# Which queue carries which half of wk: a change to the first three transfers of a gated attention and SwiGLU kernel

## The chip, the cores and the metric

The kernel runs on one core of one Trainium2 chip. The metric is the device time of one execution in microseconds; "the median" is that over several executions without a profile. The profile is of one further execution, and times in it are counted from the start of its span. The engines are called PE (TensorE; PEld is its weight load), ACT (ScalarE), DVE (VectorE), POOL (GpSimd) and SP (SyncE, which issues transfers here and computes nothing).

## The reference

The inputs are bf16. With x of 2048 rows (tokens) and 512 columns the kernel computes

```python
qkv = x @ wqkv                     # 512 x 1536, split in q, k, v; 32 heads of 16
phi = lambda t: where(t > 0, t + 1, exp(t)) + 1e-6
kv  = einsum("bhsd,bhse->bhde", phi(k), v);  z = phi(k).sum over tokens
o   = (phi(q) @ kv) / (phi(q) . z + 1e-6)
a   = o @ wo                       # linear attention
b   = (silu(x @ w1) * (x @ w3)) @ w2     # 512 -> 1376 -> 512
g   = sigmoid((x * gate_w).sum(-1))
out = g * a + (1 - g) * b
```

## The kernel before

Tokens are worked in 16 tiles of 128 (index t), four tiles to a block of 512 (index tb). Everything stays in SBUF: x in its own layout (`x_sb`), x transposed (`xT`), and all weights. The order of PE's instructions is written out by hand (`manual_schedule` for PE, line 152); on the other engines a scheduler keeps the order in which the instructions are written where nothing forces another.

**Loads.** All loads but one are issued on SP's queue (`dq = nc.sync`), in this order: the first two token tiles of x (256 KB, line 84), the second half of wk (`wk_sb[:, 2:4, :]`, 256 KB, line 86), then transposing loads of x into `xT` (lines 89 and 93) in turn with the remaining tiles of `x_sb` (line 98), then wq, the small weights, wv, w1, w3, wo and w2 (lines 99 to 114). The exception is the first half of wk (`wk_sb[:, 0:2, :]`, 256 KB, line 85), which is issued on ACT's queue. "Half" counts the four chunks of 128 input columns over which a matmul of k accumulates: the first half holds chunks 0 and 1, the second chunks 2 and 3. Behind that transfer ACT runs a one-element exp into a tile `pre` (line 88) that nothing reads: it makes ACT load its table of functions early (ACT_TABLE_LOAD).

A transfer raises a completion counter; eight counters are used in turn by all transfers, so that a later transfer on the same counter waits for the earlier one to have landed.

**The start on PE.** Nine matmuls on constants (`emit_warm`, line 163) run first; they need no transfer. Then the first two token tiles are transposed on PE itself (`emit_xT`, line 176; eight transposes, from `x_sb`), and copied to `xT` by DVE (chunks 0 and 1 of each tile, line 181) and by ACT (chunks 2 and 3, line 183). The matmuls of k for these tiles follow in this order (line 379; kc is the chunk, t the tile):

```python
for kc, t in ((0, 0), (1, 0), (0, 1), (1, 1), (2, 0), (3, 0)):
    emit_k_mm(k0[t], t, kc)
```

The first four need the first half of wk alone, the fifth is the first to need the second half. The remaining two chunks of tile 1 and the tiles 2 and 3 follow, whose `xT` comes by the transposing load of line 89.

**The rest.** phi (line 140) is an exp on ACT and two operations on DVE. For the later tiles PE takes x^T phi(k) (`emit_xp`) and the next k in turn, then q, the remainder columns, the feed-forward matmuls (`emit_ffn`) and the outputs (`emit_out`), whose results SP stores.

Of the kernel before, what the change touches and what calls it, by code (L numbers as in the profile page):

```python
# [8 lines left out]
ACT = mybir.ActivationFunctionType  # L9
ALU = mybir.AluOpType  # L10
AX = mybir.AxisListType
ENG = mybir.EngineType
FP32 = mybir.dt.float32
# [4 lines left out]
def kernel(  # L18
# [12 lines left out]
    nc = tc.nc  # L31
    P = nc.NUM_PARTITIONS

    Bb, S, D = A_x.shape
# [29 lines left out]
    x_sb = consts.tile([P, NT, D], BF16, name="x_sb")  # L64
    xT = consts.tile([P, KC, S], BF16, name="xT")
    wk_sb = consts.tile([P, KC, D], BF16, name="wk_sb")
# [9 lines left out]
    wqkv_r = A_wqkv.rearrange("(kc d) n -> d kc n", d=P)  # L76
# [3 lines left out]
    dq = nc.sync  # L80
    TF = 2
    x_first = x2d[0 : TF * P, :].rearrange("(p j) d -> p j d", j=TF)
    out_first = out2d[0 : TF * P, :].rearrange("(p j) d -> j p d", j=TF)
    dq.dma_start(out=x_sb[:, 0:TF, :], in_=x_first)
    nc.scalar.dma_start(out=wk_sb[:, 0:2, :], in_=wqkv_r[:, 0:2, D : 2 * D])
    dq.dma_start(out=wk_sb[:, 2:4, :], in_=wqkv_r[:, 2:4, D : 2 * D])
    pre = consts.tile([1, 1], FP32, name="pre")
    nc.scalar.activation(out=pre[:], in_=nc.const_aps.tensor(0.0, [1, 1], FP32), func=ACT.Exp)
    dq.dma_start(
        out=xT[:, :, TF * P : TB], in_=x2d[TF * P : TB, :], transpose=True  # L90
    )
    for tb in range(1, NTB):
        dq.dma_start(
            out=xT[:, :, tb * TB : (tb + 1) * TB], in_=x2d[tb * TB : (tb + 1) * TB, :],
# [7 lines left out]
    with nc.allow_non_contiguous_dma(reason="one gate weight per partition and chunk"):  # L102
        dq.dma_start(
            out=wr_sb[:, :, 2 * FR : NR], in_=gate_w.rearrange("(kc d o) -> d kc o", d=P, o=1)
# [7 lines left out]
    for fcs in (slice(0, FC // 2), slice(FC // 2, FC)):  # L112
# [9 lines left out]
        out=bm, in_=bm, pattern=[[-Dh, HPC], [0, Dh]], compare_op=ALU.is_ge, fill=0.0,  # L122
# [3 lines left out]
        out=bm, in_=bm, pattern=[[Dh, HPC], [0, Dh]], compare_op=ALU.is_ge, fill=0.0,  # L126
# [288 lines left out]
    for c in range(KC):  # L415
# [7 lines left out]
        out=kvT_sb[:], in0=kvT_ps[:],  # L423
# [65 lines left out]
```

## Time and profile before

| What | Value |
|---|---|
| Median of 4 executions without a profile | 179.43 us (179.22 to 179.96) |
| The profiled execution's own time | 180.21 us |
| Its span, first to last instruction | 178.4 us |
| PE busy | 173.8 us |
| ACT busy / DVE busy / POOL busy | 66.0 / 117.8 / 63.2 us |
| SP's queue: share of the 16 transfer engines' time | 30.4%, 14.72 MB |
| ACT's queue: share of the same | 0.4%, 0.26 MB |
| First x pair, issue to landing | 3.1 us |
| wk's first half, on ACT | 3.6 us |
| wk's second half, on SP | 4.0 us |

"Busy" counts the time in which an engine has an instruction in work; PE's matmuls overlap one another, so a busy PE is not PE at its peak. The profiled execution took 1.8 us more than its span, which lie around the first and last instruction. It was 0.8 us longer than the median, so differences are taken against its own time and then put on the median.

### The profile page before, as it was taken

The page shows a single profiled execution, that of the slowest core. Times are in us where ns is not written, and L with a number is a line of the kernel's source. Part 1 is how long each engine was busy: PE and PEld are TensorE (multiplying, and loading weights), DVE is VectorE, ACT ScalarE, POOL GpSimd, SP SyncE. Part 2 cuts the span into 40 slices and gives each one's busy share as a digit, 9 for nine tenths or more (in the row PEclk, how much of TensorE's full clock was granted, in tenths as well). Part 3 has the DMA queues.
Part 4 walks back from the last instruction along what each step waited for, and adds up shares of the span by engine and source line. Part 5 has one row for each costly group of instructions (what it writes and reads, how often), then busy time and mean ns, then how long its engine had stood idle before and what let it go on. Part 6 is the DMA issues. An engine that isn't in the chain of part 4 may idle for free.

```text
span 178.4 us, 2453 instructions
## 1 busy us (share of the span) xinstructions
PE 173.8 (97%) x868; PEld 84.1 (47%) x884; DVE 117.8 (66%) x203; ACT 66.0 (37%) x124; POOL 63.2 (35%) x71
## 2 busy tenths in 40 slices
PE   8999999999999999999999999999999999999993
PEld 3444444474444545444454544444545444444463
DVE  0397667898998837498786375978754669776000
ACT  3542323467532333342333333342433323341221
POOL 5087765867363323262003232620032328100000
PEclk9999999999999999999999999999999999999999
DMA  4999999921014011124000111240001022300011
GB/s 167 242 276 231 296 288 362 351 91 28 9 21 99 0 44 33 44 59 88 0 0 11 37 37 37 59 90 6 0 7 63 11 66 62 60 0 0 29 40 52
DMA packets 30252, 15.14 MB, mean 85 GB/s; under 512 B 20672, under 2 KB 30112, under 8 KB 30240
## 3 DMA queue, kind: packets, MB, share of 16 engines
q1 hardware_dynamic: 29968, 14.72, 30.4%
q10 hardware_dynamic: 272, 0.26, 0.4%
q8 instruction: 7, 0.11, 0.3%
q14 instruction: 5, 0.04, 0.1%
HBM read 8.42 MB, written 2.10 MB: 59 GB/s over the span
## 4 chain that ended last, share of the span: by engine, by line
PE 97%; issue 1%; DVE 0%; DVEq 0%
PE o_ps L357 19%; PE up_ps L320 19%; PE gate_ps L312 19%; PE o_ps L348 8%; PE XP L206 8%; PE q_ps L219 8%; PE k_ps L186 6%; PE r_ps L243 3%; PE k L186 2%; PE o_ps L352 2%; PE warm L163 2%; PE xTp L176 1%; PE kvT_ps L418 1%; PE W_ps L440 0%; PE z_ps L431 0%
## 5 line engine op out<-in xcount | busy, mean ns | idle before, releaser
L312 PE MATMUL gate_ps<-xT,w_sb 128*128 128x512 bf16 x157 | 40.8, 379 | 0.1
L320 PE MATMUL up_ps<-xT,w_sb 128*128 128x512 bf16 x157 | 40.6, 379 | 0.2
L227 POOL TENSOR_TENSOR qz<-pq,z_sb 128x512 f32<-128x512 bf16 x16 | 18.5, 1163 | 59.7 <-DVE pq L147 58.4
L325 ACT ACTIVATE th<-gate_ps 128x512 bf16<-128x512 f32 x40 | 23.9, 597 | 37.9 <-PE gate_ps L312 36.4
L357 PE MATMUL o_ps<-w_sb,hT 128*128 128x512 bf16 (+2 forms) x177 | 37.4, 355 | 0.2
L327 DVE SCALAR_TENSOR_TENSOR gs<-th,gate_ps 128x512 bf16<-128x512 bf16 x40 | 27.3, 682 | 5.6 <-ACT th L325 5.4
L330 DVE TENSOR_TENSOR hT<-up_ps,gs 128x512 bf16<-128x512 f32 x40 | 27.6, 691 | 3.8
L144 DVE TENSOR_SCALAR phi_m<-phi_e 128x512 bf16<-128x512 bf16 x32 | 14.1, 440 | 22.0 <-ACT phi_e L142 22.0
L357 PEld LDWEIGHTS <-hT 128*128 128x128 bf16 x180 | 16.8, 97 | 18.0
L320 PEld LDWEIGHTS <-w_sb 128*128 128x128 bf16 x160 | 15.6, 98 | 18.9
L312 PEld LDWEIGHTS <-w_sb 128*128 128x128 bf16 x160 | 15.6, 98 | 18.7
L362 ACT ACTIVATE o_out<-o_ps,omg 128x512 bf16<-128x512 f32 (+2 forms) x17 | 11.1, 656 | 30.4 <-PE o_ps L357 30.4
L292 POOL TENSOR_TENSOR pqn<-pq,rden 128x512 bf16<-128x512 bf16 x16 | 16.5, 1055 | 14.0 <-DVE rden L285 11.7
L196 POOL TENSOR_TENSOR pks<-pks,pk_sb 128x512 f32<-128x512 f32 x15 | 17.4, 1161 | 7.3 <-DVE pk_sb L147 6.7
L348 PE MATMUL o_ps<-W_sb,pqT 128*128 128x512 bf16 (+2 forms) x70 | 16.7, 355 | 0.1
L230 DVE TENSOR_REDUCE den<-qz 128x32 f32<-128x512 f32 x16 | 10.9, 684 | 8.6 <-POOL qz L227 8.5
L206 PE MATMUL XP<-pk_sb,x_sb 128*128 128x512 bf16 x62 | 16.2, 379 | 0.1
L219 PE MATMUL q_ps<-wq_sb,xT 128*128 128x512 bf16 x61 | 16.1, 379 | 0.1
L142 ACT ACTIVATE phi_e<-k_ps 128x512 bf16<-128x512 f32 x12 | 7.2, 597 | 14.4 <-PE k_ps L186 14.4
L142 ACT ACTIVATE phi_e<-q_ps 128x512 bf16<-128x512 f32 x16 | 9.6, 597 | 7.8 <-PE q_ps L219 6.7
L186 PE MATMUL k_ps<-wk_sb,xT 128*128 128x512 bf16 x48 | 12.3, 379 | 0.0
L147 DVE SCALAR_TENSOR_TENSOR pq<-q_ps,phi_m 128x512 bf16<-128x512 f32 x16 | 11.1, 691 | 0.5
(59 smaller groups left out, 118.5 us busy)
## 6 DMA issues: line engine op xcount, KB each, us to landing
w_sb<-in_B_w_dram SPq DMA_DIRECT2D x6, 640.0 KB, 9.7
out_dram<-o_out SPq DMA_DIRECT2D x15, 128.0 KB, 1.9
x_sb<-in_A_x_dram SPq DMA_DIRECT2D x2, 512.0 KB, 4.4
x_sb<-in_A_x_dram SPq DMA_DIRECT2D x1, 768.0 KB, 5.2
wq_sb<-in_A_wqkv_dram SPq DMA_DIRECT2D x1, 512.0 KB, 5.2
wv_sb<-in_A_wqkv_dram SPq DMA_DIRECT2D x1, 512.0 KB, 6.6
wo_sb<-in_A_wo_dram SPq DMA_DIRECT2D x1, 512.0 KB, 11.3
wk_sb<-in_A_wqkv_dram ACTq DMA_DIRECT2D x1, 256.0 KB, 3.6
```

What stands on the lines that cost most here:

```text
L186: nc.tensor.matmul(k_ps[:], lhsT=xT[:, kc, t * P : (t + 1) * P], rhs=wk_sb[:, kc, :], start=(kc == 0), stop=(kc == KC - 1),)
L196: nc.gpsimd.tensor_add(pks[:], pks[:], pk_sb[:, t, :])
L206: nc.tensor.matmul(XP_ps[dc][:], lhsT=x_sb[:, t, dc * P : (dc + 1) * P], rhs=pk_sb[:, t, :], start=(t == 0), stop=(t == NT - 1),)
L219: nc.tensor.matmul(q_ps[:], lhsT=xT[:, kc, ts_tok], rhs=wq_sb[:, kc, :], start=(kc == 0), stop=(kc == KC - 1),)
L227: nc.gpsimd.tensor_tensor(out=qz[:], in0=st[tb, "pq"][:, tt, :], in1=z_sb[:], op=ALU.mult)
L312: nc.tensor.matmul(gate_ps[:], lhsT=w1_sb[:, kc, fsl], rhs=xT[:, kc, tok_sl], start=(kc == 0), stop=(kc == KC - 1),)
L320: nc.tensor.matmul(up_ps[:], lhsT=w3_sb[:, kc, fsl], rhs=xT[:, kc, tok_sl], start=(kc == 0), stop=(kc == KC - 1),)
L325: nc.scalar.activation(out=th[:], in_=gate_ps[:], func=ACT.Tanh, scale=0.5)
L327: nc.vector.scalar_tensor_tensor(out=gs[:], in0=th[:], scalar=1.0, in1=gate_ps[:], op0=ALU.add, op1=ALU.mult)
L330: nc.vector.tensor_tensor(out=st[tb, "hT"][:, fc, :], in0=up_ps[:], in1=gs[:], op=ALU.mult)
L348: nc.tensor.matmul(o_ps[:], lhsT=st[tb, "pqT"][:, c, tsl], rhs=W_sb[:, c, a:b], start=(c == 0), stop=False,)
L357: nc.tensor.matmul(o_ps[:], lhsT=st[tb, "hT"][:, fc, tsl], rhs=w2_sb[:, fc, a:b], start=False, stop=(fc == FC - 1),)
```

## The change

The two halves of wk change queues. SP issues the first pair of x tiles and then wk's first half; ACT runs the one-element exp, with the table load ahead of it, and then issues wk's second half. A `manual_schedule` for ACT holds these in the written order. Sizes, destinations and all later transfers are the same, and no wait is added on ACT. The order of instructions of PE, DVE and POOL is the same; PE's first k matmul now waits for SP's second transfer, its fifth for ACT's.

```diff
-    dq.dma_start(out=x_sb[:, 0:TF, :], in_=x_first)
-    nc.scalar.dma_start(out=wk_sb[:, 0:2, :], in_=wqkv_r[:, 0:2, D : 2 * D])
-    dq.dma_start(out=wk_sb[:, 2:4, :], in_=wqkv_r[:, 2:4, D : 2 * D])
     pre = consts.tile([1, 1], FP32, name="pre")
-    nc.scalar.activation(out=pre[:], in_=nc.const_aps.tensor(0.0, [1, 1], FP32), func=ACT.Exp)
+    with tc.manual_schedule(engines={ENG.Activation}):
+        dq.dma_start(out=x_sb[:, 0:TF, :], in_=x_first)
+        dq.dma_start(out=wk_sb[:, 0:2, :], in_=wqkv_r[:, 0:2, D : 2 * D])
+        nc.scalar.activation(
+            out=pre[:], in_=nc.const_aps.tensor(0.0, [1, 1], FP32), func=ACT.Exp
+        )
+        nc.scalar.dma_start(out=wk_sb[:, 2:4, :], in_=wqkv_r[:, 2:4, D : 2 * D])
     dq.dma_start(
         out=xT[:, :, TF * P : TB], in_=x2d[TF * P : TB, :], transpose=True
     )
```

The lines behind the change move down by three: line 89 of the kernel before is line 92 after, line 176 is 179, line 186 is 189.

## The prediction

> **What bounds the kernel now.** I read the page first, for the engine that sets the end, and then the first microseconds of the timeline, because the change touches only the first three transfers and the table load.
>
> ```profile
> span 178.4 us, 2453 instructions
> PE 173.8 (97%) x868; PEld 84.1 (47%) x884; DVE 117.8 (66%) x203; ACT 66.0 (37%) x124; POOL 63.2 (35%) x71
> PEclk9999999999999999999999999999999999999999
> PE 97%; issue 1%; DVE 0%; DVEq 0%
> ```
>
> TensorE is busy 173.8 of 178.4 us and carries 97% of the chain that ended last. The 4.6 us that are left are 0.84 us before its first matmul, 2.9 us after its last one (the last output) and under a microsecond in between. So a delay of TensorE at the start is handed on whole to the end, and only what TensorE waits for is worth anything. The next view is the timeline from 0 (start us, duration, engine, line, operation, [idle before <- releaser]).
>
> ```profile
> 0.80 0.45 ACTq L85 DMA_DIRECT2D wk_sb<-in_A_wqkv_dram  x1
> 0.81 0.40 SPq L84 DMA_DIRECT2D x_sb<-in_A_x_dram  x1
> 0.84 3.04 PE L163 MATMUL warm<-const-bfloat16-1.0 128*128 128x512 bf16 x9 [0.84 <-PEq L473]
> ...
> 1.27 0.41 SPq L86 DMA_DIRECT2D wk_sb<-in_A_wqkv_dram  x1
> 1.28 1.28 ACT L88 ACT_TABLE_LOAD   x1 [1.28 <-PEq L473]
> ...
> 1.73 1.32 SPq L89 DMA_TRANSPOSE xT<-in_A_x_dram  x1
> ...
> 2.57 0.20 ACT L88 ACTIVATE pre<-const-float32-0.0 1x1 f32<-1x1 f32 x1
> ...
> 3.91 0.77 PEld L176 LDWEIGHTS <-x_sb 128*128 128x128 bf16 x8 [0.29 <-DMA x_sb<-in_A_x_dram]
> ...
> 4.55 0.81 ACT L183 ACTIVATE xT<-xTp 128x256 bf16<-128x256 bf16 x2 [1.78 <-PE xTp L176]
> 4.69 0.20 PEld L186 LDWEIGHTS <-xT 128*128 128x128 bf16 x2
> 4.74 4.35 PE L186 MATMUL k<-wk_sb,xT 128*128 128x512 bf16 x16
> ```
>
> Today the first half of wk leaves from ACT at 0.80 beside x on SP at 0.81, and the second half follows on SP at 1.27. The DMA view gives issue to landing (KB each, median us):
>
> ```profile
> wk_sb<-in_A_wqkv_dram ACTq DMA_DIRECT2D x1, 256.0 KB, 3.6
> x_sb<-in_A_x_dram SPq DMA_DIRECT2D x1, 256.0 KB, 3.1
> wk_sb<-in_A_wqkv_dram SPq DMA_DIRECT2D x1, 256.0 KB, 4.0
> ```
>
> So x lands at 0.81+3.1 = 3.91, wk's first half at 0.80+3.6 = 4.40, its second half at 1.27+4.0 = 5.27. TensorE takes x at 3.91, the moment it lands (the 0.29 us wait). It takes wk's first half at 4.74, 0.34 us after that landed, and wk's second half with the fifth k matmul. That one starts at 6.34, 1.07 us after the landing, as TensorE's weight loads show:
>
> ```profile
> 5.17 0.15 PEld L186 LDWEIGHTS <-xT 128*128 128x128 bf16 x1 [0.28 <-DVE xT L181]
> 5.60 0.15 PEld L186 LDWEIGHTS <-xT 128*128 128x128 bf16 x1 [0.28 <-issue]
> 6.02 0.15 PEld L186 LDWEIGHTS <-xT 128*128 128x128 bf16 x1 [0.28 <-issue]
> 6.34 1.18 PEld L186 LDWEIGHTS <-xT 128*128 128x128 bf16 x6 [0.17 <-issue]
> ```
>
> Two matmuls stand 0.43 us apart up to 6.02, and from 6.34 on six loads take 1.18 us, which is 0.22 us apart. TensorE runs its first matmuls at half rate and goes to full rate at about 6.2 in this execution, although the PEclk row reads 9 from the first slice.
>
> **The change part by part.**
> *ACT's queue.* The table load goes to the head and starts where the first ACT instruction starts now, 0.80 instead of 1.28; 1.28 us of load and 0.20 of pre then end at 2.29 instead of 2.77. ACT's next work is the xT copy at 4.55, so that costs and brings nothing; if the cover went, it would be at most the load's 1.28 us. The moved DMA issue (0.45 us) has the same cover. Neither it nor the activation before it waits for a semaphore.
>
> *When ACT's copy really leaves* is the question. No row of before has a DMA issue behind work of ACT's engine. From one side it leaves after pre ends, at 2.30. From the other, ACT's sequencer hands load and pre to the engine and goes on: a DMA issue is the sequencer's own work. Its pace is 0.03 us (issue ended at 1.25, load began at 1.28), so the issue would start at about 0.9. Two rows lie nearer to this end: pre starts 0.01 us after the load ends, so it already stood ready, and the trace's semaphore instructions of ACT, which the views leave out, stand while its engine works (one at 8.274, inside an ACTIVATE from 8.27 to 8.87). I take 0.9: "behind the table load" then holds in the program's order but not in time.
>
> *SP's queue.* x at 0.81 as now; then wk's first half in the place, size and time (1.27) of the second half now; the transposes at 1.73 and everything after keep their places. The later SP transfers that reuse these completion counters start at 11.67, long after all three have landed. POOL, DVE and TensorE keep their order; TensorE's first k matmul now waits for SP's second transfer and its fifth for ACT's.
>
> *The cost at 0.9.* The two halves of wk have changed places. ACT's copy leaves 0.1 us later than now, still 0.37 ahead of SP's second one, so it is served second again and lands about 4.5, where nobody needs it before 6.34. SP's second transfer is now the half that TensorE needs at 4.74, and by its row it lands at 5.27; 5.29 with the 0.02 of an issue. Behind the waiting matmul stand all later TensorE work and ACT's first exp; the stall is 5.29−4.74 = 0.55 us. x gains nothing, since ACT's copy runs beside it as now. Bounds of the landing: 1.27+3.6 = 4.87 (stall 0.13) and 1.27+4.0+0.1 = 5.37 (0.63). I take the row of the same queue and place.
>
> *What 0.55 us is worth.* If the rate rises at 6.2 anyway, the 0.55 us displace half-rate work: 6.2−4.74 = 1.46 us at half rate did 0.73 of full-rate work, 6.2−5.29 = 0.91 do 0.46, a loss of 0.28. If the rate is already up by 4.74, or rises later by the stall, the loss is 0.55. The profiled execution took 180.21 us, 0.78 above the median; if that is its slow start, half a microsecond per microsecond, the median one rose about 1.6 us earlier, near 4.7. Both ends are near, so I take 0.4.
>
> *The sum.* 0 (ACT) + 0 (x) + 0.4 (stall) = +0.4 on the profiled 180.21, that is 180.6; on the median, 179.43+0.4 = 179.83. Nothing later takes it back: TensorE has no wait of that size left.
>
> *A rule against the change.* The rows of ACT's and SP's first issues overlap (0.80 to 1.25 and 0.81 to 1.21), and neither is longer than SP's lone one (0.41) by more than 0.04, so no long exclusion is seen between plain copies. The Trainium skill, Perfetto Trace Analysis, section Per-instruction lifecycle, says that descriptor generation is one block that an issuing queue locks for itself until all its descriptors are made. By that, a late ACT issue falls into SP's transposes and waits them out; by the row it does not. By the rule the sum would be that of the third rival.
>
> **The rivals.**
> *1. The copy does wait for pre.* Then ACT's DMA leaves at 2.30 and wk's first half follows x at once on SP, without ACT's copy beside them. It would land as ACT's first copy does now, 4.40, bounds 4.37 (1.27+3.1) and 5.27; x could land up to 0.2 earlier of the 0.29 waited. The second half lands at 2.30+3.1 = 5.4 to 2.30+4.0 = 6.3, needed at 6.34, or at 4.74+4×0.22 = 5.6 where the rate is up early. So −0.2 to +0.3, about 179.4: not slower. For it speaks the change's wording and that ACT's work is in program order; against it the two rows above.
>
> *2. The stall keeps the clock down.* In this trace the full rate came 5.4 us after the first matmul (0.84), through one gap of 0.29 us ending at 3.91. If a gap of 0.55 begins the count anew, where 0.29 did not, the rise comes between 5.29+(6.2−3.91) = 7.6 and 5.29+5.4 = 10.7; at half rate that is (7.6−6.2)/2 = 0.7 to 2.25 us on top of 0.28: 180.4 to 181.9. Against it: TensorE would still be busy for most of that stretch. It decides from the gap length at which a stretch stops counting as busy, and no row shows that length. The skill's TensorE: Matmul & The Clock Gate, Part 1, has a free-running window of about 3.4 us that must be busy; a lost window would cost half of it, 1.7, for an estimated 181.4.
>
> *3. ACT's issue at 2.30 is held by SP's transposes.* They are issued from 1.73 to 3.05 and from 3.10 to 5.91. ACT's copy would leave at 3.05 or at 5.91, land between 6.15 and 9.9, and stall the fifth matmul by 0 to 3.6 us: 179.4 to 183.0. Against it the overlapping issues.
>
> **How the numbers follow.** Stall at half or full price 0.46; rival 1 0.30; rival 2 0.17; rival 3 0.07. I count 0.3% (0.54 us) as what a measurement of this kernel can tell from no change, its four runs lying 0.74 us apart. Slower by more than that: a third of the first (0.16), rival 2 (0.17), most of rival 3 (0.06), a little of rival 1 (0.05): 0.44. Faster by more needs more than the 0.29 us that TensorE waits for x, so only an earlier clock could do it: 0.06 out of rival 1. The same: 0.50. The likeliest case by itself reaches from 179.55 (stall 0.13) to 180.06 (0.63). The range goes down to 179.2, rival 1's low end, and up to 181.2, the middle of rival 2; about 0.06 lies below, 0.12 above.
>
> **What would show it.** Right: ACT's DMA issue before 1.3 beside the table load; an idle of about 0.5 us ahead of the first k matmul put down to the DMA of wk; that matmul near 5.3; everything after shifted by 0.3 to 0.55. Rival 1: ACT's issue at 2.3 and no idle at 4.7. Rival 2: loads 0.43 us apart beyond 7.6. Rival 3: an ACT issue much longer than 0.45, or an idle ahead of the fifth k matmul. I am wrong if the two copies are served in another order than they were issued in.

## The result and the profile after

The changed kernel is slower. The ratio of its executions to those of the kernel before is 1.0052, with a 95% interval of 1.0038 to 1.0066. The medians are 180.21 us (41 executions) and 179.61 us (65). The ratio is larger than that of the medians (1.0033) because of how the executions are spread. Of the 41, 33 lie between 179.95 and 180.69, and 8 between 181.96 and 182.47; all 65 of the kernel before lie between 179.13 and 180.46, as do its 68 further executions beside the experiments (179.13 to 180.47). So there are two losses to explain: about 0.6 us in the median of the usual executions, and 2 us more in one of five.

The profiled execution took 180.24 us. These are the lines of its page that answer to those shown of before.

```profile
span 178.5 us, 2453 instructions
PE 173.2 (97%) x868; PEld 84.0 (47%) x884; DVE 117.8 (66%) x203; ACT 66.0 (37%) x124; POOL 63.2 (35%) x71
PE 95%; DMA 2%; issue 1%; SPq 0%; DVE 0%; DVEq 0%
```

The chain that ended last now holds a DMA with 2%, which is a load of wk of 4.3 us from 1.26 on; it held none before. The timeline of the changed kernel says which one (columns as before: start, duration, engine, line, operation, idle before it).

```profile
0.80 1.28 ACT L88 ACT_TABLE_LOAD   x1 [0.80 <-PEq L476]
...
0.81 0.40 SPq L86 DMA_DIRECT2D x_sb<-in_A_x_dram  x1
...
0.86 0.43 ACTq L91 DMA_DIRECT2D wk_sb<-in_A_wqkv_dram  x1
...
1.26 0.41 SPq L87 DMA_DIRECT2D wk_sb<-in_A_wqkv_dram  x1
...
3.78 0.77 PEld L179 LDWEIGHTS <-x_sb 128*128 128x128 bf16 x8 [0.17 <-DMA x_sb<-in_A_x_dram]
...
4.56 0.10 PEld L189 LDWEIGHTS <-xT 128*128 128x128 bf16 x1
5.60 3.62 PE L189 MATMUL k<-wk_sb,xT 128*128 128x512 bf16 x16 [0.78 <-DMA wk_sb<-in_A_wqkv_dram]
5.60 3.12 PEld L189 LDWEIGHTS <-xT 128*128 128x128 bf16 x15 [0.94 <-issue]
```

ACT's copy does not leave behind the table load but 0.06 us after its start, at 0.86, while the load runs to 2.08. x is taken at 3.78 instead of 3.91. The weights for the first k matmul stand ready at 4.66, and that matmul starts at 5.60: 0.94 us of idle as the weight loads count it (0.78 from the modelled end of the last transpose), where the kernel before had none. From there on 15 weight loads take 3.12 us, 0.22 us apart, so the clock is up by the time the wait ends. How long the two copies took from issue to landing, from the views of their two lines (SP's line 87, then ACT's line 91):

```profile
L87 SPq DMA_DIRECT2D wk_sb<-in_A_wqkv_dram x1: 414/414/414, 1.3 to 1.3; - x1
...
DMA to landing us min/median/max: 4.3/4.3/4.3
```

```profile
L91 ACTq DMA_DIRECT2D wk_sb<-in_A_wqkv_dram x1: 435/435/435, 0.9 to 0.9; - x1
...
DMA to landing us min/median/max: 3.9/3.9/3.9
```

The first half of wk lands at 1.26+4.3 = 5.56 and the second, not needed until after it, at 0.86+3.9 = 4.76. The trace's packet records show the order in which the data moved: x's packets from 1.83 to 3.39 us, those of ACT's copy, issued only 0.05 us behind x, from 3.03 to 4.33, and those of SP's second copy from 3.92 to 5.02. ACT's packets do not run beside x's from the start, as they would if the two queues took even turns.

### The profile page after: what moved, and what is told of

Its sections match the earlier page's. It is cut to its first block, busy times and chain, and to the rows that moved or that the text cites. A ratio compares the mean times of both kernels' runs of the same rounds, so it can differ in the third digit from the quotient of the medians.

```text
span 178.5 us, 2453 instructions
## 1 busy us (share of the span) xinstructions
PE 173.2 (97%) x868; PEld 84.0 (47%) x884; DVE 117.8 (66%) x203; ACT 66.0 (37%) x124; POOL 63.2 (35%) x71
## 4 chain that ended last, share of the span: by engine, by line
PE 95%; DMA 2%; issue 1%; SPq 0%; DVE 0%; DVEq 0%
PE o_ps L360 19%; PE up_ps L323 19%; PE gate_ps L315 19%; PE o_ps L351 8%; PE XP L209 8%; PE q_ps L222 8%; PE k_ps L189 6%; PE r_ps L246 3%; DMA wk_sb<-in_A_wqkv_dram 2%; PE k L189 2%; PE o_ps L355 2%; PE kvT_ps L421 1%; PE W_ps L443 0%; SPq L86 0%; PE z_ps L434 0%
```

## The experiments

The theory after the result: the copies are served in the order in which they are issued; ACT's sequencer does not stop for the table load; so the half of wk that TensorE asks for first is served last, and TensorE waits for it. The idle also costs some executions a later rise of TensorE's clock. The rivals: the new place of the table load, the transposing loads that follow at once, or transfers that land late at random. Each ratio below is taken against executions of the kernel before that ran beside the experiment. Their medians differ: 179.96 us (29 executions) beside the swap alone, the load first, no copy on ACT and ACT's copy made to wait; 179.41 (17) beside the load first, again; 179.50 (21) beside the others that have a ratio. So medians are better compared with the 179.61 of the 65.

### The swap alone

```diff
+        nc.scalar.dma_start(out=wk_sb[:, 2:4, :], in_=wqkv_r[:, 2:4, D : 2 * D])
         dq.dma_start(out=wk_sb[:, 0:2, :], in_=wqkv_r[:, 0:2, D : 2 * D])
         nc.scalar.activation(out=pre[:], ..., func=ACT.Exp)
-        nc.scalar.dma_start(out=wk_sb[:, 2:4, :], in_=wqkv_r[:, 2:4, D : 2 * D])
```

> Does one part of the change alone: the two halves of wk change queues, but ACT still issues its copy (now the second half) first and loads the table behind it. Theory (the half that is issued on SP behind x is served last, and TensorE needs wk's first half earlier): the same as the changed kernel, first k matmul near 5.6 us after an idle of about 0.8 us put down to the DMA of wk, median 180.1 to 180.3 against about 179.6 of the kernel before, and some executions near 182.2. Rival (the new place of the table load or the hand-written order on ACT costs the time): no change from before, 179.5 to 179.7, first k matmul near 4.7.

Measured: 1.0046 (1.0014 to 1.0077), median 180.20, and 4 of 12 executions at 181.93 to 182.27. The timeline:

```profile
0.80 0.45 ACTq L87 DMA_DIRECT2D wk_sb<-in_A_wqkv_dram  x1
...
1.27 0.41 SPq L88 DMA_DIRECT2D wk_sb<-in_A_wqkv_dram  x1
...
5.47 3.61 PE L189 MATMUL k<-wk_sb,xT 128*128 128x512 bf16 x16 [0.46 <-DMA wk_sb<-in_A_wqkv_dram]
```

With the load in its old place the swap brings the whole loss, the executions near 182 among it.

### The load first, without the swap

```diff
-        dq.dma_start(out=wk_sb[:, 0:2, :], in_=wqkv_r[:, 0:2, D : 2 * D])
+        dq.dma_start(out=wk_sb[:, 2:4, :], in_=wqkv_r[:, 2:4, D : 2 * D])
         nc.scalar.activation(out=pre[:], ..., func=ACT.Exp)
-        nc.scalar.dma_start(out=wk_sb[:, 2:4, :], in_=wqkv_r[:, 2:4, D : 2 * D])
+        nc.scalar.dma_start(out=wk_sb[:, 0:2, :], in_=wqkv_r[:, 0:2, D : 2 * D])
```

> Does the other part alone: the table load and the one-element exp go to the head of ACT's queue, but ACT still carries wk's first half and SP its second. Theory: ACT's issue starts at 0.86 as in the changed kernel, lands 3.6 to 3.9 us later, at 4.5 to 4.8, so the first k matmul waits at most 0.2 us: 179.5 to 179.8, no executions near 182. Rival (table load placement is the cost): 180.2 with the first k matmul near 5.6.

> The version that loads the table first but leaves wk's first half on ACT, once more, because in its first measurement (0.9974 of the kernel before) the 29 runs of the kernel before had a median of 179.96 us, and 65 other runs of the same kernel had 179.61. If its gain is real (x lands some 0.1 us earlier because ACT's copy leaves 0.06 later), the ratio is 0.997 to 0.9995. If the first measurement was the luck of where the clock's rise fell, the ratio is 0.9995 to 1.001.

Measured: 0.9974 (0.9958 to 0.9990) and, the second time, 1.0004 (0.9986 to 1.0022); medians 179.45 and 179.76, none of the 24 executions over 180.21. The first k matmul starts at 4.61 and 4.62, with no idle for wk. ACT's copy lands 3.6 us after 0.86 in both.

```profile
0.86 0.43 ACTq L91 DMA_DIRECT2D wk_sb<-in_A_wqkv_dram  x1
...
4.61 3.63 PE L189 MATMUL k<-wk_sb,xT 128*128 128x512 bf16 x16
```

The place of the table load costs nothing. The gain of the first measurement did not come back in the second; the two intervals barely overlap, so no gain is claimed, and no version is shown to beat the kernel before.

### No copy on ACT

```diff
         dq.dma_start(out=wk_sb[:, 0:2, :], in_=wqkv_r[:, 0:2, D : 2 * D])
+        dq.dma_start(out=wk_sb[:, 2:4, :], in_=wqkv_r[:, 2:4, D : 2 * D])
         nc.scalar.activation(out=pre[:], ..., func=ACT.Exp)
-        nc.scalar.dma_start(out=wk_sb[:, 2:4, :], in_=wqkv_r[:, 2:4, D : 2 * D])
```

> No copy on ACT at all: x, wk's first half, wk's second half in this order on SP. Theory (copies are served in the order of their issue): x lands at 3.6 to 3.8, wk's first half (issue 1.27) near 4.4 to 4.6, the second (issue 1.73) near 5.2 to 5.5, before the fifth k matmul needs it; the transposes move by 0.46 us, which nobody notices: 179.3 to 179.7, no executions near 182. Rival (a second copy on the same queue takes 4.0 to 4.3 us to land whatever is in front of it): wk's first half lands at 5.3 to 5.6 again and the time is that of the changed kernel, 180.2.

Measured: 1.0016 (1.0001 to 1.0031), median 180.22, highest 181.03. SP's second copy, issued at 1.26 as in the changed kernel, lands 3.0 us later instead of 4.3; the third takes 4.4, to 6.13. First the view of SP's second copy, then the timeline:

```profile
L87 SPq DMA_DIRECT2D wk_sb<-in_A_wqkv_dram x1: 416/416/416, 1.3 to 1.3; - x1
...
DMA to landing us min/median/max: 3.0/3.0/3.0
```

```profile
4.53 1.49 PE L189 MATMUL k<-wk_sb,xT 128*128 128x512 bf16 x4
...
6.19 2.92 PE L189 MATMUL k<-wk_sb,xT 128*128 128x512 bf16 x12 [0.17 <-DMA wk_sb<-in_A_wqkv_dram]
...
7.21 1.41 PEld L189 LDWEIGHTS <-xT 128*128 128x128 bf16 x8 [0.49 <-DMA xT<-in_A_x_dram]
```

The same copy, on the same queue at the same time, is 1.3 us faster when no copy of ACT's stands between it and x; its packets run from 2.86 to 3.87 instead of 3.92 to 5.02. That is the clearest sign of service in order of issue. The rest of what was expected failed: the second half came at least 0.6 us later than I had said, and the transposes, pushed back by 0.5 us, were noticed (0.49 us of idle). What was won at the first half was given back there.

### TensorE asks for the halves in the order in which they land

```diff
-    for kc, t in ((0, 0), (1, 0), (0, 1), (1, 1), (2, 0), (3, 0)):
-        emit_k_mm(k0[t], t, kc)
+    for kc, t in ((2, 0), (3, 0), (2, 1), (3, 1), (0, 0), (1, 0)):
+        emit_k_mm(k0[t], t, kc, 2)     # accumulation starts at chunk 2, ends at 1
```

> The changed kernel's transfers as they are, but TensorE takes wk's second half first in the first two token tiles (chunks 2, 3 before 0, 1), so that it asks first for the half that ACT brings. The transfers still land near 4.76 (ACT) and 5.57 (SP). Theory (the time was lost only because the half that is needed first came second): the first k matmul starts at 4.75 to 4.95, where ACT's xT copies of 0.38 us now stand ahead of it, the fifth at 5.6 to 6.6 with no more than 0.2 us of idle, and the time returns to 179.3 to 179.8 with no executions near 182. Rival (something else in the transfers, such as the transposes landing later, costs it): 180.1 or more.

Measured: 1.0012 (0.9992 to 1.0033), median 179.95, none over 180.56. SP's copy still takes 4.2 us; nothing waits for it.

```profile
4.93 0.13 PEld L189 LDWEIGHTS <-xT 128*128 128x128 bf16 x2 [0.31 <-ACT xT L186]
```

The first k matmul starts at 4.93, behind ACT's xT copy as expected. With the transfers unchanged the first k matmul comes 0.67 us sooner than in the changed kernel. By the ratio most of the loss is gone; by the medians it is 0.26 of the 0.60 us (the matmul still comes 0.19 later than in the kernel before). None of the 12 was near 182, which would come by chance in 5 of 100 cases. The median is 0.15 above the range I gave.

### The idle filled

```diff
     emit_xT(1)
+    for _ in range(2):
+        nc.tensor.matmul(k0[3][:], lhsT=warm_l, rhs=warm_r, start=True, stop=True)
```

> The changed kernel with two idle matmuls on constants (128x512) between the transposes on TensorE and the first k matmul: the wait for wk stays, but TensorE is busy for 0.43 to 0.85 us of its 0.95. Theory: the usual executions stay at 180.0 to 180.4, since wk lands when it lands, and the executions near 182.2 (8 of 41) vanish, since they come from the idle costing a whole window of the clock. Rival (the executions near 182 are transfers that landed late): they stay at about one in five.

Measured: 1.0041 (1.0026 to 1.0056), median 180.29; the first k matmul again at 5.59, and none of 11 executions over 180.83. The wait's own cost stays and the executions near 182 are not seen. The changed kernel and the swap alone had 12 of 53 of these; 11 without one would come by chance in 6 of 100 cases, so by itself this is a strong hint and no more.

### The idle without the delay

```diff
-    emit_warm(TB, TB, TB, TB, TB, TB, P, P, P)
+    emit_warm(TB, TB, TB, TB)
```

> The kernel before with its warm-up cut from nine matmuls to four (from 3.0 to 1.7 us): no transfer moves and nothing is waited for longer, but TensorE is idle from about 2.55 to 3.9 instead of 3.6 to 3.9. Theory (the clock rises at the end of a window in which TensorE was busy, and an idle of over a microsecond spoils a window): x is still taken at 3.9 and the first k matmul starts at 4.74, but the clock rises later in most executions, up to 9 us: median up by 0.5 to 1.3 us, slowest executions 181.0 to 181.6. Rival (only the first matmul's start counts, or idle does not matter): 179.4 to 179.9 as before.

Measured: 1.0074 (1.0047 to 1.0101), median 181.06 of 6, up to 181.45. x lands a little earlier than before and the first k matmul starts at 4.47, sooner than in the kernel before. But TensorE's weight loads stay 0.43 us apart up to 8.3:

```profile
7.89 0.15 PEld L186 LDWEIGHTS <-xT 128*128 128x128 bf16 x1 [0.28 <-issue]
...
8.32 0.15 PEld L186 LDWEIGHTS <-xT 128*128 128x128 bf16 x1 [0.28 <-issue]
...
8.72 0.96 PEld L186 LDWEIGHTS <-xT 128*128 128x128 bf16 x5 [0.26 <-issue]
```

Nothing came late, and yet it cost over a microsecond: here an idle of TensorE in the first microseconds (0.94 us ahead of the transposes) is enough by itself to delay the rise of its clock, to 8.69.

### A plain load behind the copy instead of the transposes

```diff
+    dq.dma_start(out=x_sb[:, 3 * TPB : NT, :], in_=x_r[:, 3 * TPB : NT, :])
     dq.dma_start(
         out=xT[:, :, TF * P : TB], in_=x2d[TF * P : TB, :], transpose=True
     )
```

> The changed kernel with one plain load of x (the last four tiles, 512 KB) put on SP between wk's first half and the first transposing load; the transposes come some 1.5 us later, so the time itself is not of use, only when wk's first half lands. It is still issued at 1.26 and still served behind ACT's copy. If its late landing (4.3 us after the issue, in the changed kernel) is all a matter of being served last, it lands at 5.4 to 5.6 again. If part of it is the transposes that follow it at once and share its engines, it lands at 4.9 to 5.2, 3.6 to 3.9 us after its issue.

The load no longer stands at its later place. Measured, in one execution: 4.1 us from issue to landing, 1.27+4.1 = 5.4, against 5.56 in the changed kernel. So at most 0.2 of the 1.3 us by which this copy is late against the version without a copy on ACT comes from the transposes.

### ACT's copy made to wait

```diff
-            out=pre[:], in_=nc.const_aps.tensor(0.0, [1, 1], FP32), func=ACT.Exp
+            out=wk_sb[0:1, 2, 0:1], in_=nc.const_aps.tensor(0.0, [1, 1], FP32), func=ACT.Exp
```

> The changed kernel with one change: the one-element exp writes its result into the corner of wk's second half that the copy then overwrites, so that ACT's copy has to wait for the exp. This is rival 1 of the prediction made true. Theory: ACT's issue moves from 0.86 to about 2.3 to 2.4; SP's second transfer is then served right behind x and wk's first half lands near 4.4 instead of 5.57, so the first k matmul starts at 4.6 to 4.8 with hardly an idle; the second half lands 3.1 to 4.3 us after its issue, 5.4 to 6.7, and the fifth k matmul waits 0 to 0.6 us: 179.3 to 179.9. Rival 3 of the prediction (SP's transposing issues hold the block that makes descriptors): ACT's issue starts or ends only at 3.1 or 5.9 to 6.2, the fifth k matmul waits over 0.7 us, 180.3 or more.

Measured: 1.0273 (1.0239 to 1.0307), median 185.04. Nearly all that I had expected failed, except the issue.

```profile
1.73 1.32 SPq L91 DMA_TRANSPOSE xT<-in_A_x_dram  x1
...
2.33 0.45 ACTq L90 DMA_DIRECT2D wk_sb<-in_A_wqkv_dram  x1
...
3.09 5.96 SPq L95 DMA_TRANSPOSE xT<-in_A_x_dram  x1
...
5.95 1.02 PE L188 MATMUL k<-wk_sb,xT 128*128 128x512 bf16 x4 [1.26 <-DMA wk_sb<-in_A_wqkv_dram]
...
9.40 3.15 PE L188 MATMUL k<-wk_sb,xT 128*128 128x512 bf16 x7 [2.44 <-DMA wk_sb<-in_A_wqkv_dram]
```

ACT's issue starts at 2.33 and takes 0.45 us, right inside SP's transposing issue of 1.73 to 3.05, so it is not locked out (rival 3 of the prediction). But its copy lands 7.0 us later, at 9.36, and wk's first half, issued at 1.26, only 4.6 us later. The windows view (stretch, length, busy us of each engine, granted clock, DMA share, GB/s) shows the state of the transfers:

```profile
4.00:5.00 1.00, 0.68 (x7) 0.56 (x6) 0.58 (x2) 0.66 (x2) 0.00 (x0) 1.00 1.08 71
5.00:6.00 1.00, 0.06 (x1) 0.05 (x1) 0.00 (x0) 0.10 (x1) 0.00 (x0) 1.00 1.09 98
6.00:7.00 1.00, 0.97 (x4) 0.33 (x4) 0.00 (x0) 0.00 (x0) 0.00 (x0) 1.00 1.18 156
7.00:8.00 1.00, 0.00 (x0) 0.00 (x0) 0.00 (x0) 0.00 (x0) 0.00 (x0) 0.96 1.30 141
8.00:9.00 1.00, 0.00 (x0) 0.00 (x0) 0.00 (x0) 0.00 (x0) 0.00 (x0) 0.50 1.27 133
```

The transfer engines are fully occupied (share over 1) and move 71 to 156 GB/s. In the kernel before, the stretch from 4 to 5 us had 337. During the second wait the clock also went back to half (0.50). The packet records show what was held back of wk's first half: its data packets ended at 3.87, as in the version without a copy on ACT, but the counts that report them came up to 5.9 instead of 4.2. By these records it was the report of completion that came late, not the data.

Two further runs, of one execution each, ask what starves the copy. In the first, one plain load of 512 KB stands between wk's first half and the transposes; in the second, all three plain loads of x (1.75 MB). Their later places are empty then, and the times (183.99 and 187.32 us) say nothing about the copy.

```diff
+    for tb in range(1, NTB):      # late_copy_no_transpose; late_copy_plain: tb = 3 alone
+        dq.dma_start(out=x_sb[:, x_ts, :], in_=x_r[:, x_ts, :])
     dq.dma_start(
         out=xT[:, :, TF * P : TB], in_=x2d[TF * P : TB, :], transpose=True
     )
```

> The version in which ACT's copy waits for the exp (185.0 us; the copy left at 2.33 and landed 7.0 us later, at 9.36), with one plain load of x (512 KB) put on SP between wk's first half and the first transposing load. If the transposing packets were what starved ACT's copy and held back the landing of wk's first half (5.9), then beside a plain load ACT's copy lands 3.3 to 4.5 us after its issue, at 5.6 to 6.8, and wk's first half at 4.2 to 4.4. If ACT's queue is starved by any long load on SP, the copy lands after 8 again.

> The version in which ACT's copy waits for the exp, with all three plain loads of x (1.75 MB) on SP between wk's first half and the first transposing load. In late_copy_plain only one such load stood there, ACT's copy began to move when that load had nearly ended, and most of it again ran beside transposing packets (landing 8.49). Here it has no transposing packets beside it. If these are what starves it, the copy takes turns with plain packets, the engines keep near 350 GB/s from 4 to 8 us, and it lands at 5.6 to 7.0. If a copy on the other queue has to wait until SP's earlier loads are through, whatever they are, it lands after 8. The time itself is not of use, since the transposed x comes some 5 us late.

Measured: ACT's copy lands 6.2 us after its issue in the first (8.49) and 5.9 us in the second (8.2). wk's first half lands 3.2 and 3.0 us after its own, at 4.5 and 4.3, near the 4.2 to 4.4 expected in the first. In the second no transposing packet is near, and the engines keep their pace:

```profile
5.00:6.00 1.00, 1.00 (x4) 0.40 (x3) 0.00 (x0) 0.15 (x1) 0.00 (x0) 1.00 1.05 366
6.00:7.00 1.00, 0.44 (x2) 0.00 (x0) 0.00 (x0) 0.00 (x0) 0.00 (x0) 1.00 1.05 356
7.00:8.00 1.00, 0.00 (x0) 0.00 (x0) 0.00 (x0) 0.00 (x0) 0.00 (x0) 1.00 1.07 374
```

So the expectations of 5.6 to 6.8 and of 5.6 to 7.0 both failed: without transposes the copy still takes 2.3 us longer than ACT's row in the kernel before (3.6 us). In the second run its packets start at 4.46 and run beside those of SP's loads until 7.62; it lands at 8.2, ahead of a 512 KB load that SP issued before it (issued at 2.23, landed at 9.5). So the strict order of issue seen among the first three copies does not hold there. The two effects come apart only in part. A copy issued 1.5 us late finds SP's loads queued in front of it or beside it and lands after 8 us whatever they are. Transposing packets beside it come on top: they more than halve the rate, take the landing to 9.4, and hold back the landing of the copy ahead of them from 4.3 to 5.9. Why the mixture is so slow, and how the packets of the two queues take turns, stays open.

## Why the prediction was right, and where its sizes were off

Direction, mechanism and range held; the sum of +0.4 us was too small, and the likeliest outcome, within 0.3%, was not the one that came. Of the 0.38 us between the forecast 179.83 and the median of 180.21, 0.18 lies in the base (179.43 from four executions, 179.61 from 65) and 0.20 in the price of the stall.

*ACT's queue, 0 us:* right. The load moved to 0.80, nothing waited for it, and the load alone in the new place costs nothing.

*When ACT's copy leaves, 0.9:* right, 0.86. A value next to the row of 0.03 us between two instructions of ACT was better than the 2.30 of the written order.

*SP's second transfer is served second again and lands at 5.27:* right in kind, 0.3 us short in size; it took 4.3 us where its row said 4.0. The range that I had given for it ended at 5.37. In the four runs in which ACT's copy leaves first and SP's second is the half that is needed, it took 4.1 to 4.3; in the four in which the halves stand as in the kernel before, 4.0 to 4.1. Why the other half takes up to 0.3 longer in the same place no run shows.

*x gains nothing:* in the profiled execution x was taken 0.13 us sooner (it landed in 2.9 us instead of 3.1), and TensorE only waited longer for wk. That the change brings this is not shown: with ACT's copy issued at 0.80 x took 2.8 to 3.1 us in three traces, with it issued at 0.86 2.9 to 3.2 in six. With both, the idle is 0.94 us where I had 0.55; counted as there, from the moment at which the matmul could have started (4.61, which is 0.05 us after its weight load began, as in the kernel before), it is 0.99.

*What the stall is worth, between half and full price:* the profiles show when which price holds. The time at which the clock rose (from the trace's clock records) and the time of the same execution:

| Kernel | Clock up at | First k matmul at | Time |
|---|---|---|---|
| before | 6.23 | 4.74 | 180.21 |
| load first | 4.45 | 4.61 | 179.25 |
| load first, again | 5.70 | 4.62 | 179.90 |
| changed | 5.05 | 5.60 | 180.24 |
| swap alone | 5.16 | 5.47 | 180.19 |
| order follows landing | 6.21 | 4.93 | 180.21 |
| idle filled | 4.40 | 5.59 | 180.23 |
| idle without delay | 8.69 | 4.47 | 181.21 |
| plain load behind | 9.34 | 5.44 | 181.99 |

Without the stall an execution's time follows the clock: between the first two rows the clock comes 1.78 us sooner, of which half, 0.89, is to be won from half-rate work, and the first k matmul 0.13 us sooner, of which half, 0.07; together 0.96, as measured. With the stall, every rise before the first k matmul, at 4.40 as at 5.16, is hidden under the wait and gives 180.2. So the changed kernel pays the full price where the clock comes before 4.6, and less the later it comes, down to half of it where the clock comes after 5.6. Worked out in this way from the first row (half of each difference, and a clock up before the first k matmul counted as up at it), every other row's time comes out within 0.13 us. The two profiled executions of before and after took the same 180.2 us because the clock came 1.2 us later in the one of before. On the medians the stall cost 0.60 us, 64% of 0.94, where I had taken 73% of 0.55. The share was about right, in part by luck, since it depends on where the clock rises in each execution; the stall was mis-sized.

*Rival 2, the clock kept down, 0.17:* by all signs it happened, but in a fifth of the executions and not in all. I had given it as a case for the whole kernel; it is a share of every measurement. Its price was 0.98 to 2.53 us over the kernel before; the 8 executions lie at about 182.2, 2.6 over the median before and 2.0 over the others of the changed kernel. They carry the ratio from 1.003, the edge of my 0.3%, to 1.005. No profile fell on one of these 8, but that of the run with a plain load behind the copy has a similar idle ahead of its first k matmul (0.74 us as the weight loads count it), no other wait of note, a clock that rose at 9.34, and 181.99 us. The idle filled and the idle without delay support it from two more sides; that each of the 8 is of this kind was not seen. As an estimate from the arithmetic under the table, 182.2 us stands for a clock up near 9.4. That is 3.4 us after 6.0, and 6.0 lies among the early rises of the table (4.40 to 6.23). The Trainium skill, TensorE: Matmul & The Clock Gate, Part 1, has a free-running window of about 3.4 us. The trace agrees: in the version whose copy waits, the clock records last 3.413 us at full and 6.827 us, twice that, at half rate. How much idle such a window bears, which the prediction found in no row, the traces of these runs bound: in the 3.41 us ahead of each first rise TensorE's matmuls left at most 0.30 us of idle (in 13 traces), and in the 3.41 us before that, ahead of the two late rises, 0.58 (plain load behind) and 0.94 (idle without delay).

*Rival 1, 179.4:* it did not come, and its price was wrong by over 5 us. Made true, it cost 185.0. I had priced a copy issued at 2.30 by the rows of copies issued at 0.8 to 1.3, ahead of the transposing loads; the second half came 7.0 us after its issue instead of 3.1 to 4.0.

*Rival 3, the lock of descriptor generation:* not seen. The skill's page Perfetto Trace Analysis, Per-instruction lifecycle, has the generating block locked for one queue; here an ACT issue of 0.45 us ran inside a transposing issue of SP. The loss that the rival foresaw at that place came by another way, through the transfer engines.

## What to carry to other kernels

The written order on a queue does not put a transfer behind that engine's work: here, without a wait, ACT's sequencer issued it 0.06 us after a table load of 1.28 us had begun. So look for its place among all queues by its issue time, and give the first place to what the bounding engine asks for first. At the start of a kernel a stall of TensorE has two prices, the wait itself and the chance that its clock rises a window later, so look at the spread of the executions beside the median. A transfer's duration from a row holds only for the queues as that row found them; moved 1.5 us later, ACT's copy took 7.0 us instead of 3.9.

## What the runs showed of the hardware that I had not expected

A 256 KB copy on ACT's queue beside transposing loads on SP's moved at a joint 71 to 156 GB/s with the transfer engines fully occupied, where before the same stretch had 140 to 337. A copy issued ahead of the transposes had its landing put off, from 4.3 to 5.9 us, when another queue's copy was in flight beside them, although its data packets had ended at 3.87. And the clock rose after 3.41 us that held 0.30 us of TensorE's idle, but not after 3.41 us that held 0.58.
